# Two down-product blocks put back in two chunks, weight copies moved to ScalarE, and a new instruction order, in a four-layer attention and gated-FFN kernel

## The chip, the cores and the metric

The kernel runs on one core of a Trainium2 chip. TensorE multiplies matrices, VectorE, ScalarE and GpSimd do elementwise work, and SyncE issues the DMA transfers between HBM and the on-chip SBUF. TensorE's results go to eight PSUM banks, from which VectorE and ScalarE read them. Each engine works through its own list of instructions in order and waits at an instruction until what it needs is there. The metric is the device time of one launch in microseconds (us), lower is better; a kernel's time is the median of several runs.

## What is computed

```python
x = A_x                                              # 1 x 2048 x 576, bf16
x = x + _A_ref(_layernorm(x), A_wqkv, A_wo)
x = x + _B_ref(_layernorm(x), B_w_gate, B_w_up, B_w_down)
x = x + _A_ref(_layernorm(x), A_wqkv, A_wo)          # the same weights again
x = x + _B_ref(_layernorm(x), B_w_gate, B_w_up, B_w_down)
```

`_layernorm` is over the 576 features, without scale or shift. `_A_ref` projects to q, k and v for 32 heads of 18; token s attends to the 8 tokens s, s-2, ..., s-14, and the result goes through `wo`. `_B_ref` is `((x @ w_gate) * (x @ w_up)) @ w_down`, with an inner width F of 4608 and no nonlinearity. In tiles of 128 there are 16 token tiles and 36 f tiles; 576 features are four full tiles and a rest of 64.

## The kernel before

**Chunks.** The work goes through in chunks of tokens, called j in the code. Chunk 0 is the first token tile of the first attention layer, chunk 1 the second tile; chunks 2, 3 and 4 are pairs of tiles (256 tokens); the rest are pairs too, combined into stages of 512 tokens for the FFN. While TensorE works on the FFN of one chunk (or stage), the attention of later chunks is fitted in: `IN_GU` (L1466) says at which unit of a chunk's FFN which chunk's projection begins.

**Attention** (`attention`, L563). `head` (L441) makes the layernorm: statistics on VectorE (L455, L457) or ScalarE, `rstd` on ScalarE (L461, L462), and the apply on ScalarE (L473, L474) or on VectorE (L479). `LN1_V` and `LN2_V` say for which chunks VectorE does the apply of the first and the second layernorm. The projection is L638 for chunks 0 and 1 and L590 for the others. Scores are VectorE products of q and shifted k (L784), summed over the head by matmuls with a selection matrix `Esel` (L800) for chunks 0 and 1, or by a trip through DRAM (`s_dram`, L846, L849). The softmax is VectorE and ScalarE work (L827 to L895) and ends in the weights `a_c`. For chunks below 4 these are spread over the heads' rows by matmuls (L908) and copied to `ab`; for the later ones `a_c` goes out to `a_dram` (L921) and comes back in four pieces as `ab` (L924), on SyncE's queue. Then the a·v products: for chunk 0 pairs of offsets (L939), summed by TensorE (L979, L980) and scaled by 1/sum (L1004, L1008; the sum's matmuls stand behind product number `SPZ`); for the others one product and one sum per offset on VectorE (L954 or L957, and L963), or in pairs where the chunk is in `PAIR`. The output product with `wo` is L512 for chunks 0 and 1 and L1027 for the others, followed by the residual (L1033) and the second layernorm (`head` again; for chunks 0 and 1 `tail_fast` L500, statistics at L515).

**Weights.** In the first layer the columns of `wqkv` are put in another order on the chip (`permute`, L360). The value columns come last (`late_v`, L384): five large copies of 128 x 512 elements, one for each tile of 128 features, on the engine that `VENG` names, and five small ones on GpSimd; all are L373.

**FFN.** A unit (`g_unit`, L1136) is two to four f tiles of gate and up: full tiles at L1144, the rest of 64 features at L1154. ScalarE copies the gate result (L1085) or the up result (L1087), VectorE multiplies (L1079, L1101), and the product stays in SBUF as `hb` or in spare buffers. `Down` (L1163) multiplies with `w_down`: `block` (L1189) takes two f tiles and, for each token tile, issues a matmul of 512 columns (L1204) and one of 64 (L1205) per f tile; `fetch` (L1172) loads the weights in a ring of six buffers `wd` (L317), always a fixed number of blocks ahead; `close` (L1216) adds the sums to the residual. `first_pair` (L1309) does chunks 0 and 1 together, `small` (L1355) chunks 2, 3 and 4, `big` (L1386) the later stages. In `small`, chunks 3 and 4 (`inter`) have 18 units and 18 blocks, and the blocks run along with the units: before unit u = 4, 6, ..., 16 stand blocks u-4 and u-3, which are blocks 0 to 13. The loop after the last unit begins at nu - 2 = 16, so blocks 14 and 15 (f tiles 28 to 31 of 36) are left out of the down product of these two chunks, although their gate and up products are made and their weights loaded:

```python
        for u in range(nu):
            begin_units(in_gu.get(u, ()), push)
            if inter and u % 2 == 0 and u > 2:
                for b in (u - 4, u - 3):
                    dn.block(b)
            push(g_unit(range(u * fpu, (u + 1) * fpu), xT, xk, n, hblk[homes[u]], f"hm{homes[u]}", True))
        push()
        for b in range(nu - 2 if inter else 0, NFT // 2):
```

**The order.** Nothing of the order is written by hand. Every step is an `op` of `Plan` (L21) with an engine, an estimated cost, the tiles that it reads and writes, and a priority. `run` picks, again and again, the operation that could start earliest by these estimates (then by priority, then by age), appends it to its engine's list, and moves the estimated clock of that engine. Operations of chunk 0 are marked `first`: another operation is taken only if it would not delay one of those that are ready (`soon`), with an allowance per engine (`wait`). Gaps on TensorE before the first FFN matmul are filled with up to 44 dummy matmuls (`warm`, L1041 to L1043). So a change in costs, priorities or rules can move any instruction on any engine.

Of the kernel before, what the change touches and what calls it, by code (L numbers as in the profile page):

```python
# [20 lines left out]
class Plan:  # L21
# [52 lines left out]
    def run(self, slots):  # L74
        clock = {e: 0.0 for e in self.LAT}
        dma = 0.0
        free = {k: [(0.0, i) for i in range(v)] for k, v in slots.items()}
        cand = [o for o in self.ops if o.n == 0]
        done = 0
        while cand:  # L80
            best, found, soon = None, [], {}
            for o in cand:
                t = 0.0
                for p in o.deps:
                    e = p.ready if p.eng != o.eng or p.nbytes and p in o.data else p.end
                    if e > t:
                        t = e
                t += o.margin
                if o.hold is not None:
                    f = free[o.hold]  # L90
                    if not f:
                        continue
                    t = max(t, min(f)[0])
                if o.pair is not None:
                    if len(free["unit"]) < len(o.pair):
                        continue
                    f = sorted(free["unit"])[:len(o.pair)]
                    t = max([t, f[0][0]] + [x[0] + 150 - o.lead for x in f[1:]])
                if o.need is not None:
                    t = max(t, o.need["at"])  # L100
                t = max(t, clock[o.eng])
                found.append(((t, o.prio, o.idx), o))
                if o.first:
                    soon[o.eng] = min(t, soon.get(o.eng, t))
            for key, o in sorted(found, key=lambda x: x[0]) if self.warm is not None else ():
                if o.first or soon.get(o.eng, 1e12) >= key[0] + o.cost - self.wait.get(o.eng, 0):
                    best = (key, o)
                    break
            if best is None and found:
                best = min(found, key=lambda x: x[0])  # L110
            assert best is not None, "the plan is stuck"
            (t, _, _), o = best
            cand.remove(o)
            if o.hold is not None:
                got = min(free[o.hold])
                free[o.hold].remove(got)
                o.use["slot"] = got[1]
            if o.pair is not None:
                for u in o.pair:
                    got = min(free["unit"])  # L120
                    free["unit"].remove(got)
                    u["at"], u["slot"] = got
            if o.eng == "PE" and self.warm is not None:
                if o is self.cool:
                    self.warm = None
                else:
                    self.warm(min(44, int(max(0, t - clock["PE"] - 100) / 100)))
            o.end = t + o.cost
            clock[o.eng] = o.end
            o.ready = o.end + o.lat  # L130
            if o.nbytes:
                dma = max(dma, o.end) + o.nbytes / (330.0 if dma < 60000 else 250.0)
                o.ready = dma + o.land
# [12 lines left out]
        assert done == len(self.ops)  # L146
# [3 lines left out]
def kernel(  # L150
# [32 lines left out]

    NWD = 6
    KENG = {1: ("ACT", "ACT"), 2: ("ACT", "DVE"), 3: ("ACT", "ACT"), 4: ("ACT", "POOL")}
    VENG = ('POOL', 'POOL', 'ACT', 'ACT', 'ACT')
    LN1_PE, LN2_PE, ATT_PE, LN2_V, L1_LATE, MG, MGD = 3, 2, 4, 3, 4, 200, 2500
    LN1_V = (0, 1, 2)
    LN1_S, LN2_S = (), (2, 3, 4, 5)
    SPZ, TREE, PAIR, HPAIR = 3, (1,), (0,), 1  # L190
    RAW = 2
    WAIT = {"PE": 1e+09, "DVE": 1e+09, "ACT": 1e+09}
    PRE, SUM_PE = '', 2
# [362 lines left out]
        b, o = order_sc.index((la, t0 // NSC)) % 2, t0 % NSC  # L556
        return xnT_B[b][:, :, o * P:(o + nst) * P], [f"xB{b}_{o + i}" for i in range(nst)]

    LN1P = {1: 1.6, 2: 2, 3: 3, 4: 3, 5: 2.5, 6: 1.5, 7: 3, 8: 3}
    ATP = {1: 2.5, 2: 2.5, 3: 2.5, 4: 1.5, 5: 1.5, 6: 1.5}  # L560
    LPP = {1: 3, 2: 1.5, 3: 1.5, 4: 2, 5: 2, 6: 3}

    def attention(j, la, t0, nst, units=None, pre=""):  # L563
        fast = j == 0
# [367 lines left out]
        def pr_(i):  # L932
            return late["prod"][i][:, :, :, 0:n]
# [22 lines left out]
            abw = late["ab"][:, :, 0:W * sq].rearrange("p j (w s) -> p j w s", w=W)[:, :, i_].unsqueeze(1).to_broadcast([P, KT, 4, sq])  # L956
            nc.vector.tensor_tensor(js(dst), js(vs), abw, op=ALU.mult)  # L957
        for i_ in range(0 if j in PAIR else W):
            o = op("DVE", 60 + 3 * n, lambda i_=i_: one_v(i_), r=vk + abk, w=[f"pq{i_ % 2}"] if i_ else ok, prio=prio,
                   margin=0 if on_pe or i_ else 800 if j < 5 else 3500)  # L960
            pl.also(o, ["prod1"])
            if i_:
                op("DVE", 60 + 3 * n, lambda i_=i_: nc.vector.tensor_tensor(oT[:, :, 0:n], oT[:, :, 0:n], pr_(1)[:, i_ % 2], op=ALU.add),  # L963
                   r=[f"pq{i_ % 2}"], w=ok, prio=prio)
        for g in range(W // 2 if j in PAIR and not fast else 0):
            to = 1 if g or not tree else 0
# [388 lines left out]
    def small(j, inter, in_gu, in_d):  # L1355
        self_pair["on"] = HPAIR and not inter
        la, t0, nst = seq[j]
        n, fpu = nst * P, 4 // nst
        nu = NFT // fpu
        homes = [14 + u % 4 for u in range(nu)] if inter else [*range(9, 14), *range(9), *range(14, 18)]  # L1360

        def lhs(ft, i):
            o = (ft % fpu) * n + i * P
            return hblk[homes[ft // fpu]][:, o:o + P]
        dn = Down(t0, nst, list(range(NFT)), lhs, lambda ft, i: f"hm{homes[ft // fpu]}", la == n_al - 1, False, 2)
        dn.fetch(len(wd_ring))
        push = pusher(2, 1) if inter else pusher(3)
        marks["ld"], marks["ld1"] = marks.get("ld1"), chain["pe"]
        xT, xk = place(la, t0, nst)
        if j > 2:  # L1370
            next(gens[j], None)
        if j == 3:
            hand_over("pa", (1,))
# [4 lines that stand above are left out]
                    dn.block(b)  # L1378
            push(g_unit(range(u * fpu, (u + 1) * fpu), xT, xk, n, hblk[homes[u]], f"hm{homes[u]}", True))
        push()  # L1380
        for b in range(nu - 2 if inter else 0, NFT // 2):
            insert_d(in_d.get(b, ()))
            dn.block(b)
        dn.close()
# [78 lines left out]
        else:  # L1463
            next(gens[2], None)
    pl.first = False
    IN_GU, IN_D = {0: {3: [2]}, 2: {0: [3], 8: [4]}, 3: {0: [5], 9: [6]}}, {}  # L1466
    first_pair(IN_GU[0], IN_D.get(0, {}))
    for j in (2, 3, 4):
        small(j, j > 2, IN_GU.get(j, {}), IN_D.get(j, {}))
# [38 lines left out]
```

## Time and profile before

| what | us |
|---|---|
| median of 3 runs | 1047.61 |
| all runs | 1047.61, 1046.82, 1049.3 |
| the profiled execution | 1049.22 |
| its span in the profile | 1047.4 |

The busy times on the profile's page are 1027.5 us for TensorE, 716.7 us for VectorE, 459.3 us for ScalarE and 13.5 us for GpSimd; the time between the span and the execution's own time, 1.8 us, is outside the profile.

How rows are read. In a timeline a row has the start and the duration in us, engine, line, operation, what is written and read, the shapes and the number of instructions merged into it; in brackets at the end stands how long the engine was idle before it and what ended that. Matmuls overlap, so their pitch is read from start to start and not from the duration. A waits row has total, number and longest. A row of a stretch has its ends and length, the busy time and count of TensorE, its weight loads, VectorE, ScalarE and GpSimd, the granted TensorE clock, the DMA share and GB/s. SPq is SyncE's DMA issue.

### The profile page before, as it was taken

What the parts mean: (1) busy time and instruction counts of PE and PEld (TensorE: products, weight loads), DVE (VectorE), ACT (ScalarE), POOL (GpSimd) and SP (SyncE); (2) the same over time, 40 slices, a digit from 0 to 9 for tenths busy, and PEclk for the clock granted to TensorE, in tenths of its full rate; (3) what the DMA queues carried; (4) which work ended last, traced back from release to release, by engine and by line L of the source; (5) the groups of instructions that cost most, each with busy time, mean ns of one, the idle gap of its engine ahead of it and who ended that gap; (6) DMA issues with size and microseconds to landing.
All of it is one profiled execution on the core that took longest, in us unless ns stands there. A gap on an engine that the chain in (4) does not pass through costs nothing.

```text
span 1047.4 us, 19571 instructions
## 1 busy us (share of the span) xinstructions
PE 1027.5 (98%) x7890; PEld 597.6 (57%) x8008; DVE 716.7 (68%) x1327; ACT 459.3 (44%) x935; POOL 13.5 (1%) x51
## 2 busy tenths in 40 slices
PE   7999999999999999999999999999999999999998
PEld 6886876776765445554455544564455644554444
DVE  8886787877849886497776968579684696832211
ACT  5564764644745651354424543154531444214420
POOL 4000000000000000000000000000000000000000
PEclk9999999999999999999999999999999999999999
DMA  8918218355653715355143641525436342454212
GB/s 264 333 40 195 61 42 241 78 138 171 153 146 101 209 30 158 115 153 183 38 137 93 188 134 49 158 69 181 133 85 156 100 164 88 118 155 136 69 49 88
DMA packets 142539, 136.16 MB, mean 130 GB/s; under 512 B 46064, under 2 KB 140144, under 8 KB 142448
## 3 DMA queue, kind: packets, MB, share of 16 engines
q1 hardware_dynamic: 142448, 134.91, 44.7%
q8 instruction: 62, 1.02, 0.4%
q14 instruction: 29, 0.24, 0.1%
HBM read 114.49 MB, written 10.88 MB: 120 GB/s over the span
## 4 chain that ended last, share of the span: by engine, by line
PE 95%; DMA 2%; issue 1%; DVE 1%; SPq 1%; POOL 0%; ACT 0%; DVEq 0%
PE pu L1144 19%; PE pg L1144 18%; PE pu L1204 9%; PE pg L1204 7%; PE pa L1144 6%; PE pg L590 5%; PE pu L590 5%; PE acct L1144 5%; PE pa L1204 4%; PE pu L1154 3%; PE pg L1154 2%; PE pg L1205 2%; PE acct L1204 1%; PE acct L1027 1%; PE pu L1205 1%; PE pu L1027 1%
## 5 line engine op out<-in xcount | busy, mean ns | idle before, releaser
L1144 PEld LDWEIGHTS <-reg 128*128 128x128 bf16 x3072 | 277.9, 98 | 222.1 <-issue 24.2
L1144 PE MATMUL pu<-xnT_B,reg 128*128 128x512 bf16 (+2 forms) x1282 | 226.1, 315 | 1.5 <-issue 0.5
L1144 PE MATMUL pg<-xnT_B,reg 128*128 128x512 bf16 (+2 forms) x1192 | 213.7, 318 | 1.1 <-issue 0.3
L1204 PEld LDWEIGHTS <-reg 128*128 128x128 bf16 x864 | 84.5, 98 | 98.2
L1101 DVE TENSOR_TENSOR reg<-reg,g_sb 128x512 bf16<-128x512 bf16 x144 | 60.0, 419 | 90.5 <-ACT reg L1087 90.0
L1085 ACT CAST g_sb<-pu 128x512 bf16<-128x512 f32 x119 | 70.0, 589 | 87.8 <-PE pg L1154 41.0
L590 PEld LDWEIGHTS <-wqkv 128*128 128x128 bf16 (+1 forms) x1050 | 88.0, 97 | 34.3 <-issue 18.4
L784 DVE TENSOR_TENSOR prod<-qT,kT 128x2560 bf16<-128x2560 bf16 (+1 forms) x68 | 97.1, 1431 | 10.0 <-ACT kT L711 8.9
L1085 ACT CAST g_sb<-pg 128x512 bf16<-128x512 f32 x100 | 58.9, 590 | 96.4 <-PE pu L1154 37.7
L963 DVE TENSOR_TENSOR qT<-qT,prod 128x1280 bf16<-128x1280 bf16 (+1 forms) x112 | 89.8, 801 | 2.7
L1205 PEld LDWEIGHTS <-reg 128*128 128x128 bf16 x864 | 84.7, 98 | 1.9
L957 DVE TENSOR_TENSOR prod<-vT,ab 128x1280 bf16<-128x1280 bf16 x91 | 73.9, 818 | 4.8 <-DMA ab<-a_dram 4.8
L1144 PE MATMUL pa<-xnT_B,reg 128*128 128x512 bf16 (+1 forms) x325 | 75.0, 356 | 0.2
L461 ACT ACTIVATE rstd<-mv,eps_t 128x2 f32<-128x2 f32 (+1 forms) x32 | 9.5, 296 | 148.4 <-DVE mv L457 148.0
L590 PE MATMUL pg<-xnT_A,wqkv 128*128 128x256 bf16 (+1 forms) x495 | 71.7, 273 | 0.1
L590 PE MATMUL pu<-xnT_A,wqkv 128*128 128x256 bf16 (+1 forms) x465 | 70.5, 273 | 0.0
L1204 PE MATMUL pu<-wd,reg 128*128 128x512 bf16 x259 | 70.5, 380 | 0.0
L1154 PE MATMUL pg<-xnT_B,reg 64*128 64x512 bf16 (+2 forms) x302 | 62.7, 317 | 0.4
L1154 PE MATMUL pu<-xnT_B,reg 64*128 64x512 bf16 (+2 forms) x327 | 61.5, 315 | 0.3
L1144 PE MATMUL acct<-xnT_B,reg 128*128 128x512 bf16 (+1 forms) x217 | 56.6, 375 | 0.6 <-issue 0.2
L1205 PE MATMUL pg<-wd,reg 128*128 128x64 bf16 x264 | 50.9, 193 | 0.8
L1154 PEld LDWEIGHTS <-reg 64*128 64x128 bf16 x768 | 29.9, 94 | 36.0 <-issue 24.0
(256 smaller groups left out, 1489.8 us busy)
## 6 DMA issues: line engine op xcount, KB each, us to landing
wd<-in_B_w_down_dram SPq DMA_DIRECT2D x152, 288.0 KB, 3.2
reg<-in_B_w_gate_dram SPq DMA_DIRECT2D x24, 768.0 KB, 4.6
reg<-in_B_w_up_dram SPq DMA_DIRECT2D x24, 768.0 KB, 6.2
reg<-in_B_w_down_dram SPq DMA_DIRECT2D x28, 288.0 KB, 3.2
s_dram<-s SPq DMA_DIRECT2D x13, 512.0 KB, 3.2
rg<-s_dram SPq DMA_DIRECT2D x52, 128.0 KB, 3.0
ab<-a_dram SPq DMA_DIRECT2D x52, 128.0 KB, 2.8
reg<-in_B_w_gate_dram SPq DMA_DIRECT2D x24, 96.0 KB, 5.5
```

The costliest lines, as they stand in the source:

```text
L461: nc.scalar.activation(rstd[:, 0:nst], mv[:, 0:nst, 1], ACT.Ln, bias=eps_t[:], scale=1.0 / D if act else 1.0)
L590: nc.tensor.matmul(ring[use[p_]["slot"]][0:m, e * n:(e + 1) * n], lhsT=wqkv[r_, k, c0:c0 + m], rhs=xnT_A[r_, k, 0:n], start=start, stop=st ...
L784: nc.vector.tensor_tensor(late["prod"][lp(p_)][:, :, :, 0:n], q2, k2, op=ALU.mult)
L957: nc.vector.tensor_tensor(js(dst), js(vs), abw, op=ALU.mult)
L963: op("DVE", 60 + 3 * n, lambda i_=i_: nc.vector.tensor_tensor(oT[:, :, 0:n], oT[:, :, 0:n], pr_(1)[:, i_ % 2], op=ALU.add), r=[f"pq{i_ % 2 ...
L1027: nc.tensor.matmul(b()[:, 0:HD], lhsT=oT[:, t, i * P:(i + 1) * P], rhs=wo_p[:, t, hh * HD:(hh + 1) * HD], start=(t == 0), stop=(t == KT - 1))
L1085: op("ACT", 590, lambda: nc.scalar.copy(g_sb[gs][:, 0:ul], bk(0)[:, 0:ul]), r=[keys[0]], w=[f"g{gs}"], prio=0, **fg)
L1101: op("DVE", 410, lambda: nc.vector.tensor_tensor(dst, dst, g_sb[gs][:, 0:ul], op=ALU.mult), r=[f"g{gs}"], w=[dk], prio=0)
L1144: nc.tensor.matmul(ring[use[q]["slot"]][:, e * n:(e + 1) * n], lhsT=w_[:, k], rhs=xT[:, k], start=(first and k == 0 and e == 0), stop=(las ...
L1154: nc.tensor.matmul(ring[use[q]["slot"]][:, e * n:(e + 1) * n], lhsT=w_[r_], rhs=xT[r_, KF], start=(fresh and e == 0), stop=not fresh, skip ...
L1204: nc.tensor.matmul(bank_of(i)[:, 0:cut], lhsT=lhs, rhs=wt[:, ft % 2, 0:cut], start=first and not plus, stop=last_)
L1205: nc.tensor.matmul(tail_of(i), lhsT=lhs, rhs=wt[:, ft % 2, cut:D], start=(first and not plus and (self.fin or i == 0)), stop=last_, skip_g ...
```

## The change

1. **Blocks put back**: the loop after the units begins at nu - 4 = 14 for chunks 3 and 4, so that blocks 14 and 15 are multiplied: 8 more matmuls of 512 columns and 8 of 64 for each of the two chunks. Loads stay as many.
2. **Copies**: all five large copies of the value weights are ScalarE's; before, the first two were GpSimd's.
3. **Layernorm**: the second apply of chunk 2 goes from VectorE to ScalarE (`LN2_V` 3 to 2).
4. **Chunk 0 and 1**: the matmuls of chunk 0's softmax sum stand behind its second product instead of its fourth (`SPZ`); chunk 1's a·v is done in pairs of offsets (`PAIR`): 4 products, 3 sums of 1280 elements and a last one of 640 in place of 8 products and 7 sums of 640. `L1_LATE` 4 to 2 names which of chunk 1's score products (L784, by its pair of feature tiles) is held until chunk 0's FFN input is on its way (L806).
5. **Order**: new estimated costs for the a·v steps, new priorities (`LN1P`, `ATP`, `LPP`), chunk 4's projection begun one unit earlier (unit 7), and a new rule in `run`: for chunk 0's operations that are not yet issued, ready or not, it estimates the earliest start along their chain, so that other work is kept from delaying those too.

In the new lists TensorE has 5 fewer dummy matmuls and 32 more of the down product; the three groups of score sums of chunk 1 that stood ahead of the first FFN matmul stand behind it; chunk 2's `wo` product stands behind 54 pairs of the running down product instead of 34; and the store of `a_c` to `a_dram` in chunk 3's FFN stands behind four loads of `wd` instead of six.

```diff
@@ Plan.run
         cand = [o for o in self.ops if o.n == 0]
+        lead, gone = [o for o in self.ops if o.first], set()
...
                 if o.first:
                     soon[o.eng] = min(t, soon.get(o.eng, t))
+            if self.warm is not None:
+                est = {}
+                for o in lead:
+                    t = 0.0
+                    for p in o.deps | o.order:
+                        e = p.end + p.lat if p in gone else est.get(p, 0.0)
+                        t = e if e > t else t
+                    soon[o.eng] = min(max(t, clock[o.eng]), soon.get(o.eng, 1e12))
+                    est[o] = t + o.cost + o.lat
...
             cand.remove(o)
+            gone.add(o)
+            if o.first:
+                lead.remove(o)
@@ settings
-    VENG = ('POOL', 'POOL', 'ACT', 'ACT', 'ACT')
-    LN1_PE, LN2_PE, ATT_PE, LN2_V, L1_LATE, MG, MGD = 3, 2, 4, 3, 4, 200, 2500
+    VENG = ('ACT', 'ACT', 'ACT', 'ACT', 'ACT')
+    LN1_PE, LN2_PE, ATT_PE, LN2_V, L1_LATE, MG, MGD = 3, 2, 4, 2, 2, 200, 2500
...
-    SPZ, TREE, PAIR, HPAIR = 3, (1,), (0,), 1
+    SPZ, TREE, PAIR, HPAIR = 1, (1,), (0, 1), 1
...
-    LN1P = {1: 1.6, 2: 2, 3: 3, 4: 3, 5: 2.5, 6: 1.5, 7: 3, 8: 3}
-    ATP = {1: 2.5, 2: 2.5, 3: 2.5, 4: 1.5, 5: 1.5, 6: 1.5}
-    LPP = {1: 3, 2: 1.5, 3: 1.5, 4: 2, 5: 2, 6: 3}
+    LN1P = {1: 2.5, 2: 1.5, 3: 1.5, 4: 2, 5: 3, 6: 1, 7: 1.5, 8: 3}
+    ATP = {1: 3, 2: 3, 3: 2.5, 4: 3, 5: 2.5, 6: 2}
+    LPP = {1: 2, 2: 3, 3: 3, 4: 1.5, 5: 3, 6: 2.5}
@@ attention, a·v one offset at a time (product, and sum)
-            o = op("DVE", 60 + 3 * n, lambda i_=i_: one_v(i_), ...
+            o = op("DVE", 80 + 2.7 * n, lambda i_=i_: one_v(i_), ...
-                op("DVE", 60 + 3 * n, lambda i_=i_: nc.vector.tensor_tensor(oT[:, :, 0:n], ...
+                op("DVE", 80 + 2.7 * n, lambda i_=i_: nc.vector.tensor_tensor(oT[:, :, 0:n], ...
@@ small
-        for b in range(nu - 2 if inter else 0, NFT // 2):
+        for b in range(nu - 4 if inter else 0, NFT // 2):
@@ projections inside the FFN
-    IN_GU, IN_D = {0: {3: [2]}, 2: {0: [3], 8: [4]}, 3: {0: [5], 9: [6]}}, {}
+    IN_GU, IN_D = {0: {3: [2]}, 2: {0: [3], 7: [4]}, 3: {0: [5], 9: [6]}}, {}
```

More of the change, by code (lines that the diff above doesn't have):

```diff
@@ L958, in attention @@
         for i_ in range(0 if j in PAIR else W):
-            o = op("DVE", 60 + 3 * n, lambda i_=i_: one_v(i_), r=vk + abk, w=[f"pq{i_ % 2}"] if i_ else ok, prio=prio,
+            o = op("DVE", 80 + 2.7 * n, lambda i_=i_: one_v(i_), r=vk + abk, w=[f"pq{i_ % 2}"] if i_ else ok, prio=prio,
                    margin=0 if on_pe or i_ else 800 if j < 5 else 3500)
@@ L962, in attention @@
             if i_:
-                op("DVE", 60 + 3 * n, lambda i_=i_: nc.vector.tensor_tensor(oT[:, :, 0:n], oT[:, :, 0:n], pr_(1)[:, i_ % 2], op=ALU.add),
+                op("DVE", 80 + 2.7 * n, lambda i_=i_: nc.vector.tensor_tensor(oT[:, :, 0:n], oT[:, :, 0:n], pr_(1)[:, i_ % 2], op=ALU.add),
                    r=[f"pq{i_ % 2}"], w=ok, prio=prio)
```

## The prediction

> **What bounds the kernel now.** I read the shares of the chain that ended last, then the list of what TensorE waited for, then the busy time by stretch.
>
> ```profile
> PE 95%; DMA 2%; issue 1%; DVE 1%; SPq 1%; POOL 0%; ACT 0%; DVEq 0%
> ```
> ```profile
> PE pg L638 <- POOL wqkv L373: 2.7, 2, 2.2
> PE pa L1204 <- DVE hb L1079: 2.0, 1, 2.0
> ...
> PE pg L638 <- ACT xnT_A L495: 1.0, 1, 1.0
> ...
> PE pg L1204 <- DVE hb L1079: 0.2, 1, 0.2
> ```
> ```profile
> 0.00:34.00 34.00, 27.24 (x468) 23.15 (x469) 28.51 (x64) 18.69 (x42) 12.94 (x43) 0.95 0.94 280
> ...
> 175.00:250.00 75.00, 72.61 (x670) 53.93 (x676) 58.78 (x104) 39.58 (x84) 0.00 (x0) 1.00 0.54 142
> 250.00:330.00 80.00, 79.27 (x672) 55.52 (x681) 59.28 (x124) 46.72 (x98) 0.00 (x0) 1.00 0.49 121
> 330.00:1020.00 690.00, 684.42 (x4332) 343.19 (x4416) 459.97 (x845) 271.46 (x537) 0.00 (x0) 1.00 0.41 122
> ```
>
> 95% of the chain is TensorE. A waits line gives microseconds in total, times, and the longest. A stretch line gives its length, then busy time of TensorE, its weight loads, VectorE, ScalarE and GpSimd, the granted clock and DMA. TensorE is idle 6.8 us of the first 34 us and about 5.6 us of the 690 us after 330. So the time is TensorE's own work plus two places: the start, where one chain of small steps runs before the first gated FFN matmul, and one wait of 2.0 us at L1204. An added matmul costs its full pitch unless it falls into one of these holes; a gain on VectorE or ScalarE counts only in them.
>
> **The blocks put back (L1381).** The loop after the units begins at block 14 instead of 16, for chunks 3 and 4. A block is 2 f tiles by 2 token tiles, each one matmul of 512 and one of 64 columns: 8 pairs for two blocks, 16 in all. The price is read from another two-block step of chunk 3, on TensorE's own timeline:
>
> ```profile
> 218.29 0.38 PE L1204 MATMUL pa<-wd,hb 128*128 128x512 bf16 x1
> ...
> 220.25 1.04 PE L1144 MATMUL pu<-xnT_B,reg 128*128 128x256 bf16 x8
> ```
>
> From 218.29 to 220.25 is 1.96 us for 8 pairs, 0.245 us a pair. Sixteen pairs: **+3.92 us** if nothing covers them. The weights of these blocks are loaded already, so no transfer is added.
>
> At the end of chunk 3 the new pairs come right after the last unit's matmuls, ahead of blocks 16 and 17, and there is the hole (TensorE, then VectorE):
>
> ```profile
> 241.83 1.04 PE L1144 MATMUL pu<-xnT_B,reg 128*128 128x256 bf16 x8
> 244.84 0.39 PE L1204 MATMUL pa<-wd,hb 128*128 128x512 bf16 x1 [1.97 <-DVE hb L1079]
> ```
> ```profile
> 237.42 0.43 DVE L1079 TENSOR_TENSOR hb<-hb,g_sb 128x512 bf16<-128x512 bf16 x1 [1.16 <-ACT hb L1087]
> 242.16 1.56 DVE L957 TENSOR_TENSOR prod<-vT,ab 128x1280 bf16<-128x1280 bf16 x2 [4.31 <-DMA ab<-a_dram]
> 243.63 0.82 DVE L957 TENSOR_TENSOR qT<-vT,ab 128x1280 bf16<-128x1280 bf16 x1
> 244.37 0.42 DVE L1079 TENSOR_TENSOR hb<-hb,g_sb 128x512 bf16<-128x512 bf16 x1
> ```
>
> The 237.42 product is unit 15's, so blocks 14 and 15 have their operands 5 us before TensorE is free at 242.87. Unit 16's product, at 244.37, stands on VectorE behind three multiplications that waited 4.31 us for the attention weights. So the two blocks fill 1.96 of 1.97 us: **−1.97 us**, even if the wait's end stays where it is. At the end of chunk 4 the same happens to the smaller wait:
>
> ```profile
> 304.11 0.39 PE L1204 MATMUL pg<-wd,hb 128*128 128x512 bf16 x1 [0.16 <-DVE hb L1079]
> ```
>
> **−0.16 us.** Is 244.8 itself moved? The weights came late through SyncE's queue (VectorE, then the queue, then the chain):
>
> ```profile
> 229.34 0.69 DVE L895 TENSOR_TENSOR a_c<-Lt,zs 128x512 bf16<-128x512 f32 x1
> ```
> ```profile
> 219.47 13.08 SPq L317 DMA_DIRECT2D wd<-in_B_w_down_dram  x6
> 232.64 0.42 SPq L921 DMA_DIRECT2D a_dram<-a_c  x1
> ```
> ```profile
> 236.91 5.22 DMA ab<-a_dram
> ```
>
> `a_c` was ready at 230.03, its store issued at 232.64: six loads of down weights stood ahead for 13.08 us. Since nothing read the weights of the missing blocks, their buffers were loaded again at once; in the changed order only four such loads stand ahead of the store. So I expect the store some 2.5 us earlier and the wait gone with room. If the queue stays as it is, the blocks still just cover it; if the store came later, each us would cost one. Range of both blocks together: +1.8 (covered, my value) to +3.92.
>
> **The start.** The large value-weight copies go from GpSimd to ScalarE (L373). GpSimd's, ScalarE's, TensorE's and VectorE's rows:
>
> ```profile
> 11.46 4.51 POOL L373 COPY wqkv<-xl 128x64 bf16<-128x64 bf16 x7 [1.49 <-DMA xl<-in_A_wqkv_dram]
> ```
> ```profile
> 11.65 3.13 ACT L373 COPY wqkv<-xl 128x512 bf16<-128x512 bf16 x3
> ```
> ```profile
> 14.39 0.40 PE L638 MATMUL pg<-xnT_A,wqkv 128*128 128x128 bf16 x4 [2.21 <-POOL wqkv L373]
> ...
> 17.50 0.31 PE L638 MATMUL pu<-xnT_A,wqkv 128*128 128x128 bf16 x1
> ...
> 33.48 1.07 PE L1144 MATMUL pg<-xnT_B,reg 128*128 128x128 bf16 x16
> ```
> ```profile
> 19.18 0.42 DVE L840 TENSOR_REDUCE mx<-acct 128x32 f32<-128x256 f32 x1 [0.63 <-PE acct L800]
> ...
> 24.49 0.63 DVE L479 TENSOR_SCALAR xn<-xf,mv,rstd 128x576 bf16<-128x576 bf16 x2
> ...
> 27.94 0.29 DVE L1004 TENSOR_TENSOR oT<-pg,Lt 128x128 bf16<-128x128 f32 x1 [0.70 <-PE pg L980]
> 28.39 0.76 DVE L1008 TENSOR_TENSOR oT<-acct,Lt 128x256 bf16<-128x256 f32 x2 [0.16 <-issue]
> 29.07 0.82 DVE L784 TENSOR_TENSOR prod<-qT,kT 128x1280 bf16<-128x1280 bf16 x1
> ```
>
> Three copies on ScalarE took 3.13 us, 1.04 each; five end at 11.65 + 5.2 = 16.9. The first is there at 12.7 instead of after 14, so the 2.21 us wait goes, but the last one now sets the end: the value product's last piece starts at about 16.9 instead of 17.5, and the softmax's first reduction at 18.6 instead of 19.18: 0.6 us. On VectorE, the layernorm apply at 24.49 (0.63 us, L479) stands between chunk 0's a·v products; in the changed order it comes behind the last of them, where VectorE had a pause of 0.70 us anyway: 0.65 us. And L784 for chunk 1 leaves its place behind L1008, 0.82 us, of which I count 0.35, since the wo product of TensorE lies beside it. Sum: **−1.6 us** to the first FFN matmul at L1144. Three groups of 20 score-sum matmuls (L800), 0.26 us each, that stand ahead of 33.48 move behind it too, so the first L1144 itself should come 2.4 us earlier, and 0.8 of that is paid later. Bounds: 0 (the last copy, at 16.9, could hold everything) to −3.5 (2.7 of waits and 0.82).
>
> A clock effect lies in this stretch:
>
> ```profile
> 16.54 0.63 PE L638 MATMUL pg<-xnT_A,wqkv 128*128 128x128 bf16 x4
> ...
> 21.30 0.39 PE L638 MATMUL pg<-xnT_A,wqkv 128*128 128x128 bf16 x4
> ```
> ```profile
> 16.00:16.50 0.50, 0.47 (x5) 0.47 (x6) 0.50 (x1) 0.00 (x0) 0.00 (x0) 0.50 0.32 55
> ...
> 20.00:20.50 0.50, 0.00 (x0) 0.00 (x0) 0.50 (x3) 0.50 (x2) 0.00 (x0) 1.00 1.07 390
> ```
>
> The granted clock is 0.50 at 16.0 and 1.00 at 20.0; four matmuls take 0.63 us in the one and 0.39 in the other. The Trainium skill, "TensorE: Matmul & The Clock Gate", Part 1, says that the gate looks at free-running windows of about 3.4 us and gives half rate after an idle one. That agrees with these rows, and it speaks against the change: a new order moves the idle pieces against the windows. I keep it as a rival.
>
> **The middle: chunk 2, and the rest of the new order.** Chunk 1's eight products and seven sums (640 columns) become four, three and one of double width, as many elements; its a·v ends within 1 us of before, 0.6 us ahead of need: 0 ± 0.6. Chunk 4's projection is begun a unit earlier: 0, TensorE is full there and does the same work. One second layernorm apply of chunk 2 goes from VectorE to ScalarE, about 1.4 us ahead of its reader: 0. What I can't cost at nothing is the wo product of chunk 2 (VectorE, then TensorE):
>
> ```profile
> 75.02 0.82 DVE L954 TENSOR_TENSOR qT<-vT,ab 128x1280 bf16<-128x1280 bf16 x1 [0.28 <-ACT ab L711]
> ...
> 82.94 0.69 DVE L1079 TENSOR_TENSOR xnT_B<-xnT_B,g_sb 128x1024 bf16<-128x1024 bf16 x1 [0.52 <-ACT xnT_B L1087]
> ...
> 88.32 0.82 DVE L963 TENSOR_TENSOR qT<-qT,prod 128x1280 bf16<-128x1280 bf16 x1
> ```
> ```profile
> 90.45 0.78 PE L1027 MATMUL acct<-wo_p,qT 128*128 128x288 bf16 x5
> ```
>
> Before, the 15 products and sums began at 75.02 among the FFN products and ended at 89.1, 1.3 us ahead of L1027. In the changed order they stand behind the last FFN product (about 82, 1.6 us earlier than 83.6): 15 × 0.79 = 11.9 gives 93.9. L1027 is moved behind 20 more pairs of the down product, 4.9 us: 90.45 − 1.6 + 4.9 = 93.75. Slack is −0.1: I take +0.3 us, with 0 to +3 (four of the 0.79 us steps later) as its range.
>
> **Sum**: 3.92 − 1.97 − 0.16 − 1.6 + 0.3 = +0.5 us. On the profiled execution, 1049.22 us with a span of 1047.4, that gives 1049.7; the three runs have their median at 1047.61 (1046.82 to 1049.3), 1.6 below it, so the forecast is **1048.1 us**.
>
> **The rivals.** *Chunk 2's wo product becomes the wait* (slower). For it: VectorE is the fuller engine there, and 11.9 us now follow each other with no slack at L1027. Against: 20 more pairs stand ahead of L1027, which cover the later start but for 0.1 us. It decides once `qT` is done later than 93.75; each VectorE step pushed ahead costs 0.79, and layernorm, on ScalarE now, hands it on. Three or four steps, 2.4 to 3.2: about 1050.8. *The half clock comes again* within chunk 0's a·v stretch, since TensorE's new order has a half-idle piece at 19 to 22 us. The 0.63 against 0.39 above, over 3.4 us, is some 1.3 to 1.7 us: 1049.6. The Trainium skill ("TensorE: Matmul & The Clock Gate", Part 1) has this by its rule. *The start gives all* (faster): both waits for GpSimd, 2.7 us, and the 0.82 come through, −3.5 instead of −1.6, and chunk 2's wo product waits for nothing, 0 instead of +0.3: 1048.1 − 1.9 − 0.3 = 1045.9; with one or two of the pauses left behind the softmax (0.70 at 27.94) filled too, 1045.2. For it: the chain is serial; against: the last copy at 16.9. *The blocks don't fit the hole*, because the changed queue holds unit 15's or the weights' arrival: 3.92 in full and a wait behind, about 1050.2.
>
> **How the numbers follow.** Forecast 1048.1, own range 1046.7 to 1049.5: 0.48. Wo product of chunk 2: 0.20. Start gives all: 0.20. Half clock: 0.06. Blocks not covered: 0.06. A measurement can tell about 0.2%, 2.1 us, from no change: 1045.5 to 1049.7. Faster: two thirds of the start's case and a small tail of the forecast, 0.16. Slower: nine tenths of the wo product's case, most of the uncovered blocks, half of the clock's case and a tail of the forecast, 0.30. The rest, 0.54, is within. The range is 1044.8 to 1051.2: 1 in 10 is left out on each side.
>
> **What would show it.** Right: L1204 and L1205 with 16 more pairs; no wait of TensorE for L1079 near 243 us; the store of `a_c` near 230 and no row of six down-weight loads before it; first FFN matmul (L1144's line) near 31.1 us; the wait for GpSimd's copies gone, and none above 0.5 us for chunk 2's `qT`. Wrong: a wait at the wo product near 93 us; a granted clock of 0.50 after 22 us; a first FFN matmul later than 33; a wait of over 1 us at the end of chunk 3; or a changed pitch after 330 us, which no term here allows.

## The result, and the profile after

Against before on the same chip the change makes the kernel slower: 1051.35 us against 1048.05 us (medians of 8 runs each), a ratio of 1.0026 with a 95% interval of 1.0015 to 1.0037. The unchanged pair was measured once more (e11): 1050.17 against 1047.55, ratio 1.0021 (1.0012 to 1.0030). So it costs 2.2 to 2.7 us, where the forecast was +0.5. Among the runs of e11 and of before beside it whose mean granted clock was 1.000 the difference is larger, 3.6 us, since 15 of the 21 runs of before had a lower clock and only 4 of the 11 of the changed kernel (0.999). The two profiled executions show little of it: 1049.77 us with a span of 1048.0, against 1049.22 and 1047.4.

First, what TensorE waited for after (total, times, longest; the line numbers are 13 higher, so L1217 is the old L1204, L1040 the old L1027, L386 the old L373).

```profile
...
PE acct L813 <- DVE prod L797: 1.2, 2, 1.0
PE pa L1056 <- ACT xnT_A L508: 1.1, 1, 1.1
PE pu L603 <- issue: 1.0, 1, 1.0
...
PE pu L921 <- ACT a_c L884: 0.6, 1, 0.6
PE pg L1157 <- DMA reg<-in_B_w_gate_dram: 0.5, 1, 0.5
PE pu L651 <- POOL wqkv L386: 0.4, 1, 0.4
...
```

The wait for GpSimd's copies (2.7 us) is down to 0.4, both waits for L1079 are gone, and no wait for chunk 2's `wo` product has come. New is 1.0 us of "issue" at a projection matmul, time in which TensorE waited for nothing that the profile names. The same stretches as before:

```profile
0.00:34.00 34.00, 28.45 (x514) 24.78 (x514) 26.16 (x64) 21.72 (x46) 11.16 (x41) 1.00 0.98 288
...
175.00:250.00 75.00, 74.58 (x688) 55.30 (x695) 60.62 (x106) 40.20 (x86) 0.00 (x0) 1.00 0.51 145
250.00:330.00 80.00, 79.37 (x673) 55.09 (x683) 55.66 (x119) 45.71 (x96) 0.00 (x0) 1.00 0.51 117
330.00:1020.00 690.00, 684.32 (x4330) 343.17 (x4415) 458.88 (x845) 271.44 (x537) 0.00 (x0) 1.00 0.42 122
```

From 330 us on TensorE's busy time is the same to 0.1 us. At the end of chunk 3's FFN, SyncE's queue, VectorE and TensorE show the mechanism that was forecast: `a_c` is ready at 228.88 (the end of the L908 row), its store goes out at once with no loads ahead of it, the products follow 4 us earlier than in the profile before, and blocks 14 to 17 run through without a pause (these are the first and the last rows of their 512-column matmuls in TensorE's timeline).

```profile
228.92 0.34 SPq L934 DMA_DIRECT2D a_dram<-a_c  x1
```
```profile
228.19 0.69 DVE L908 TENSOR_TENSOR a_c<-Lt,zs 128x512 bf16<-128x512 f32 x1
...
238.00 1.56 DVE L970 TENSOR_TENSOR prod<-vT,ab 128x1280 bf16<-128x1280 bf16 x2 [1.18 <-DMA ab<-a_dram]
```
```profile
241.68 0.38 PE L1217 MATMUL pa<-wd,hb 128*128 128x512 bf16 x1
...
245.11 0.38 PE L1217 MATMUL pg<-wd,hb 128*128 128x512 bf16 x1
```

Of chunk 2's a·v, the first and the last VectorE row, and TensorE's `wo` product behind it:

```profile
82.13 0.82 DVE L967 TENSOR_TENSOR qT<-vT,ab 128x1280 bf16<-128x1280 bf16 x1
...
93.28 0.82 DVE L976 TENSOR_TENSOR qT<-qT,prod 128x1280 bf16<-128x1280 bf16 x1
```
```profile
94.33 0.78 PE L1040 MATMUL acct<-wo_p,qT 128*128 128x288 bf16 x5
```

The start of the changed kernel, ScalarE's copies, VectorE's softmax and the first FFN matmul:

```profile
11.88 5.22 ACT L386 COPY wqkv<-xl 128x512 bf16<-128x512 bf16 x5
```
```profile
17.07 0.40 DVE L853 TENSOR_REDUCE mx<-acct 128x32 f32<-128x256 f32 x1
...
25.33 0.74 DVE L1021 TENSOR_TENSOR oT<-pu,Lt 128x256 bf16<-128x256 f32 x2
27.38 0.47 DVE L528 BATCH_NORM_STATS2 st<-acct 128x6 f32<-128x288 f32 x1 [1.30 <-PE acct L525]
```
```profile
30.17 1.05 PE L1157 MATMUL pg<-xnT_B,reg 128*128 128x128 bf16 x16 [0.46 <-DMA reg<-in_B_w_gate_dram]
```

Five copies in 5.22 us, as worked out; the softmax comes 2.1 us earlier than before, the first FFN matmul 3.3 us earlier. Then where did the gain go? To compare kernels below, I use one ruler: the start of the n-th full FFN matmul (L1144's line) in each trace. Matmul 513 comes after the start and the FFN of chunks 0 and 1, 1025 near the end of chunk 3's units, 1401 in the stage behind chunk 4; the two places of the change lie between the last two.

| profile | 1st | 513th | 1025th | 1401st | 1025 to 1401 |
|---|---|---|---|---|---|
| before | 33.48 | 113.44 | 238.56 | 334.39 | 95.83 |
| before again, e9 | 33.47 | 113.43 | 238.55 | 332.47 | 93.92 |
| before again, e10 | 33.68 | 113.65 | 238.77 | 333.03 | 94.26 |
| after | 30.17 | 112.42 | 237.54 | 334.87 | 97.33 |
| after again, e11 | 30.89 | 112.57 | 238.02 | 335.56 | 97.54 |

From matmul 1401 to the last one every kernel takes 673.40 us, to 0.01. (Some matmul records are missing from the traces; counted by weight loads, of which none is missing, the differences between the kernels in the last column are the same to 0.01.)

### The profile page after: what moved, and what is told of

Read it like the earlier page. It is cut to its first block, busy times and chain, and to the rows that moved or that the text cites. A ratio compares the mean times of both kernels' runs of the same rounds, so it can differ in the third digit from the quotient of the medians.

```text
span 1048.0 us, 19612 instructions
## 1 busy us (share of the span) xinstructions
PE 1030.1 (98%) x7917; PEld 599.3 (57%) x8035; DVE 710.7 (68%) x1317; ACT 463.6 (44%) x941; POOL 11.7 (1%) x49
## 4 chain that ended last, share of the span: by engine, by line
PE 96%; DMA 2%; issue 1%; POOL 1%; SPq 0%; DVE 0%; ACT 0%; POOLq 0%
PE pu L1157 19%; PE pg L1157 18%; PE pg L1217 9%; PE pu L1217 6%; PE pa L1157 6%; PE pg L603 5%; PE pu L603 5%; PE acct L1157 4%; PE pa L1217 4%; PE acct L1217 3%; PE pu L1167 3%; PE pg L1167 3%; PE pg L1218 2%; PE pu L1040 1%; PE pu L1218 1%; DMA reg<-in_B_w_gate_dram 1%
## 5 line engine op out<-in xcount | busy, mean ns | idle before, releaser
L1157 PE MATMUL pg<-xnT_B,reg 128*128 128x512 bf16 (+2 forms) x1200 | 220.6, 319 | 1.9 <-issue 0.6
L1217 PEld LDWEIGHTS <-reg 128*128 128x128 bf16 x864 | 84.5, 98 | 98.2
L1098 ACT CAST g_sb<-pu 128x512 bf16<-128x512 f32 x113 | 66.5, 590 | 104.2 <-PE pg L1167 59.1
L1098 ACT CAST g_sb<-pg 128x512 bf16<-128x512 f32 x111 | 65.5, 590 | 76.5 <-PE pu L1167 44.1
L976 DVE TENSOR_TENSOR qT<-qT,prod 128x1280 bf16<-128x1280 bf16 x105 | 86.3, 822 | 2.3
L1167 PE MATMUL pg<-xnT_B,reg 64*128 64x512 bf16 (+2 forms) x305 | 68.2, 319 | 0.6
L1217 PE MATMUL pg<-wd,reg 128*128 128x512 bf16 (+1 forms) x233 | 62.7, 369 | 0.0
L1218 PE MATMUL pg<-wd,reg 128*128 128x64 bf16 x320 | 61.7, 193 | 0.7
L1157 PE MATMUL acct<-xnT_B,reg 128*128 128x512 bf16 (+1 forms) x213 | 54.1, 375 | 0.1
L1167 PEld LDWEIGHTS <-reg 64*128 64x128 bf16 x768 | 29.9, 94 | 36.4 <-issue 24.6
```

What stands on the lines that cost most here:

```text
L976: op("DVE", 80 + 2.7 * n, lambda i_=i_: nc.vector.tensor_tensor(oT[:, :, 0:n], oT[:, :, 0:n], pr_(1)[:, i_ % 2], op=ALU.add), r=[f"pq{i_ % ...
L1098: op("ACT", 590, lambda: nc.scalar.copy(g_sb[gs][:, 0:ul], bk(0)[:, 0:ul]), r=[keys[0]], w=[f"g{gs}"], prio=0, **fg)
L1157: nc.tensor.matmul(ring[use[q]["slot"]][:, e * n:(e + 1) * n], lhsT=w_[:, k], rhs=xT[:, k], start=(first and k == 0 and e == 0), stop=(las ...
L1167: nc.tensor.matmul(ring[use[q]["slot"]][:, e * n:(e + 1) * n], lhsT=w_[r_], rhs=xT[r_, KF], start=(fresh and e == 0), stop=not fresh, skip ...
L1217: nc.tensor.matmul(bank_of(i)[:, 0:cut], lhsT=lhs, rhs=wt[:, ft % 2, 0:cut], start=first and not plus, stop=last_)
L1218: nc.tensor.matmul(tail_of(i), lhsT=lhs, rhs=wt[:, ft % 2, cut:D], start=(first and not plus and (self.fin or i == 0)), stop=last_, skip_g ...
```

## The experiments

The theory at the outset: the start's gain is real only against executions whose clock was halved there, and one of the two pairs of blocks is covered. The rival: the start gains what was forecast, and the blocks cost more.

**e1: the blocks alone.** The kernel before with

```diff
-        for b in range(nu - 2 if inter else 0, NFT // 2):
+        for b in range(nu - 4 if inter else 0, NFT // 2):
```

> The kernel before with only the loop start changed, so that blocks 14 and 15 are multiplied in chunks 3 and 4. Theory (one of the two places is covered): at the end of chunk 3 the 1.96 us fill the wait of 1.97 us, at the end of chunk 4 there is only 0.16 us to fill, so +1.8 us on before, ratio 1.0017. Rival (the blocks are not covered): +3.9 us, ratio 1.0037, with a wait at L1204 still there near 244 us.

Measured: 1050.34 us against 1048.32, ratio 1.0020 (1.0007 to 1.0033), +2.1 us. In the profile the wait near 244 us is gone, and the store of `a_c` goes out at 229.43, right behind `a_c` (228.72 + 0.69). So the queue's order follows from the blocks alone, as forecast. The interval holds +1.8 and leaves the rival's +3.9 out. This speaks for the theory only for now: e8 to e10 and e12 below show what the blocks cost and how much was covered. (In e1, and in e8 and e12 below, the planner also moves other work behind the added blocks.)

**e2: all but the blocks.** The changed kernel with

```diff
-        for b in range(nu - 4 if inter else 0, NFT // 2):
+        for b in range(nu - 2 if inter else 0, NFT // 2):
```

> The changed kernel with the loop start of before: blocks 14 and 15 of the down product of chunks 3 and 4 are left out again, all else as changed. Theory (the new start gains only against executions in which the clock was halved at the start, as in the profiled one of before): full-clock runs 0.5 to 1.0 us slower than full-clock runs of before, so ratio 1.000 to 1.001. Rival (the start gains 1.6 us as forecast, and the blocks cost more): 1.2 us or more faster than before, ratio 0.9988.

This leaves blocks 14 and 15 out of chunks 3 and 4, as before does. Measured: 1047.98 against 1048.32, ratio 0.9995 (0.9983 to 1.0007): neither a clear gain nor a loss; the interval holds both theories' values. Its profile has the wait of 1.0 us at the same projection matmul, and at the end of chunk 3 a wait of 0.76 us, for down weights, where before's profile had 1.97. The runs at a mean clock of 1.000 do tell the two apart: the six of e2 have a median of 1048.07 and begin at 1047.65, the ten of before have 1046.76 and end at 1047.18. So at equal clock the new order without the blocks is 1.3 us slower. The theory has the direction right there, with 0.5 to 1.0, and the rival, 1.2 us faster, fails; over all runs the two are level because before lost clock in 25 of its 35 runs.

**e3 and e4: more dummy matmuls**, in before and in after:

```diff
-                    self.warm(min(44, int(max(0, t - clock["PE"] - 100) / 100)))
+                    self.warm(min(80, int(max(0, t - clock["PE"] - 100) / 65)))
```

> The kernel before with more dummy matmuls in the same gaps of TensorE (one for each 65 ns of an estimated gap instead of one for each 100, at most 80). Theory (the runs of before near 1049.3 us are those whose clock was halved for one window of 3.4 us at the start): fewer or no runs with a mean clock of 0.998, and those with a full clock near 1047.4; median 0.3 to 0.8 us lower. Rival (the two groups of runs come from something else, or the dummies stand in the way): the same spread of 1046.8 to 1049.8, or all runs later by the dummies.

> The changed kernel with the same denser dummy matmuls. Theory (clock): no run with a mean clock of 0.998, and the median falls from 1051.35 to near 1050.0, where the full-clock runs of the changed kernel are. Rival (the runs near 1051.5 come from the late instruction fetch that the profile shows as a wait of 1.0 us near 39.8 us, which two runs at full clock speak for): the runs near 1051.4 stay, at a clock of 1.0.

Measured: 1050.99 (ratio 1.0025, 1.0013 to 1.0037) and 1051.22 (1.0022, 1.0011 to 1.0033). The mean clock was 1.000 in 8 of e3's 12 runs and in all 12 of e4's, so the runs agree with dummies holding it up, but the kernels are no faster for it: e3's 513th matmul stands at 114.47 us at full clock, before's at 113.44 with a halved one, and e4's at 114.11, after's at 112.42. The rival's second half holds, the dummies stand in the way. What the clock costs can be read from the 35 runs of before beside these: median 1046.76 for the 10 at a mean clock of 1.000, 1048.47 for the 12 at 0.998, and 1050.45 for the 6 at 0.995. A step down goes with 1.7 to 2.0 us here, and with 0.8 to 2.5 in the two later sets of before. It doesn't hold run by run: in e5 below the five runs at 0.998 are no slower than the five at 1.000 (1049.43 and 1049.85), and e10, at 1.000, took longer than e9 at 0.998. And both profiles have the wait for "issue", of 0.91 us, e3's in before's order.

**e5: fewer dummies.** The wait for "issue" stands at one and the same place in the profiles of four kernels (after, e2, e3, e4), the 1217th row of TensorE's list (weight loads counted), in whatever line that is. The changed kernel with

```diff
-                    self.warm(min(44, int(max(0, t - clock["PE"] - 100) / 100)))
+                    m = min(44, int(max(0, t - clock["PE"] - 100) / 100), 96 - self.warmed)
+                    self.warmed += m
+                    self.warm(m)
```

> The changed kernel without the last 16 of its 112 dummy matmuls (those after 20.47 us), all other work in the same order. Theory (TensorE's instructions from its 1217th row on arrive at a set time, about 39.8 us, since in the four profiles with a wait of 0.9 to 1.0 us near 38 to 40 us it stands at just that row; 32 rows less ahead of it bring TensorE there about 1.8 us of matmuls later): no such wait, full-clock runs 1.0 us faster than those of the changed kernel (1050.31), near 1049.4. Rival (the wait belongs to a time or to the weights that are loaded then): it stays, and the time is within 0.4 us of the changed kernel's; the clock may be halved more often.

Measured: 1049.85 against 1048.41, ratio 1.0012 (1.0002 to 1.0021); the changed kernel's ratios are 1.0026 and 1.0021, so by the medians e5 is about 1 us ahead of it, but the intervals overlap. The wait is gone (TensorE's timelines of after, then of e5, around that row; e5's line numbers are 3 higher):

```profile
38.45 0.38 PE L603 MATMUL pu<-xnT_A,wqkv 128*128 128x256 bf16 x2
39.84 0.38 PE L603 MATMUL pu<-xnT_A,wqkv 128*128 128x256 bf16 x2 [1.00 <-issue]
```
```profile
39.85 0.60 PE L606 MATMUL pg<-xnT_A,wqkv 128*128 128x256 bf16 x4
40.29 0.60 PE L606 MATMUL pu<-xnT_A,wqkv 128*128 128x256 bf16 x4
40.73 0.38 PE L924 MATMUL pa<-a_c,Bsel 128*128 128x256 bf16 x2
```

The theory is right about the wait. The gain of 1.0 us is not shown: at a mean clock of 1.000 e5 has 1049.85 (5 runs) against the changed kernel's 1050.31 (5 runs), half of it, and in e5's profile, whose clock was halved for one window, the 513th matmul stands at 112.65, no earlier than after's 112.42. Of the kernels that compute all blocks e5 has the lowest ratio, but its interval overlaps e1's too; it is still behind before, which leaves two blocks of two chunks out.

**e6 and e7: the copies.** e6 is the changed kernel with the first two copies on GpSimd, e7 the kernel before with all five on ScalarE:

```diff
-    VENG = ('ACT', 'ACT', 'ACT', 'ACT', 'ACT')
+    VENG = ('POOL', 'POOL', 'ACT', 'ACT', 'ACT')
```

```diff
-    VENG = ('POOL', 'POOL', 'ACT', 'ACT', 'ACT')
+    VENG = ('ACT', 'ACT', 'ACT', 'ACT', 'ACT')
```

> The changed kernel with the first two large value-weight copies on GpSimd again. Theory (the copies on ScalarE shorten the waits at the start by 1 to 2 us, but most of what the profiled kernel before lost there was its halved clock): full-clock runs 0 to 0.6 us slower than the changed kernel's 1050.3, and more runs with a mean clock of 0.998 or less, as TensorE waits longer in one piece. Rival (forecast: the copies give at least the 0.6 us of the softmax and the whole waits of 2.7 us count): 1.5 us or more slower at full clock.

> The kernel before with all five large value-weight copies on ScalarE, nothing else. Theory: full-clock runs within 0.6 us of before's 1046.8, fewer runs at 0.998 or less, so that the median falls by some 0.5 to 1 us. Rival: 1.6 us faster at full clock too.

Measured: e6 1053.82 (1.0053, 1.0041 to 1.0065), by the ratios 2.8 to 3.4 us behind the changed kernel; its 513th matmul stands at 115.17, 2.75 later than after's. A part of that is the clock, which was below 1.000 in four of its five runs, the profiled one among them, as the theory said it would be; the one run at 1.000 took 1052.56, 2.25 more than the changed kernel's median there. So the theory's 0 to 0.6 us fell, and the forecast's reading is borne out, by one run at full clock: in the new order the copies on ScalarE are worth some 2 to 3 us, near the 2.7 that the waits said. (The planner also gave the other steps of the start another order.) e7, though, took 1066.69 (1.0173, 1.0160 to 1.0186). Neither theory had that; its 513th matmul stands at 132.44, 19.0 later than in the profile of before. The copies change the estimated clocks, and the planner put the scores of chunk 2 (45.9 to 59.0 us) in the middle of chunk 1's a·v on VectorE, while TensorE's list has chunk 2's score sums and spreads ahead of the rest (TensorE's timeline, then stretches of e7):

```profile
55.91 0.30 PE L800 MATMUL pa<-s,Esel 128*32 128x128 bf16 x4 [2.93 <-DVE s L794]
59.08 0.30 PE L800 MATMUL pa<-s,Esel 128*32 128x128 bf16 x4 [2.87 <-DVE s L794]
64.90 0.59 PE L908 MATMUL acct<-a_c,Bsel 128*128 128x512 bf16 x1 [5.51 <-DVE a_c L895]
```
```profile
50.00:56.00 6.00, 3.07 (x62) 2.83 (x60) 5.76 (x10) 1.18 (x3) 0.00 (x0) 0.97 0.85 292
56.00:70.00 14.00, 4.28 (x21) 2.06 (x21) 13.09 (x29) 3.88 (x9) 0.00 (x0) 0.53 0.00 1
```

TensorE did 4.28 us of work in 14, and the granted clock fell to 0.53. So part 2 of the change and its new rule, priorities and costs are not separate gains: the copies alone, under the old planner's settings, lose 18 us. Which of the planner's settings prevents that was not tried.

**e8: the blocks of chunk 3 alone**, in before:

```diff
-        for b in range(nu - 2 if inter else 0, NFT // 2):
+        for b in range((nu - 4 if j == 3 else nu - 2) if inter else 0, NFT // 2):
```

> The kernel before with blocks 14 and 15 put back in chunk 3 alone; chunk 4 still leaves them out. Theory (the wait of 1.97 us at the end of chunk 3 takes them): within 0.3 us of before, and no wait at L1204 near 243 us; all of what e1 lost is then chunk 4's. Rival (both chunks cost alike): about half of what both blocks cost together in e1, 1.0 us or more.

This kernel leaves blocks 14 and 15 of chunk 4 out. Measured: 1049.84 against 1048.41, ratio 1.0016 (1.0005 to 1.0027), by the ratio +1.7 us; the rival's value. Yet by the ruler 1025 to 1401 takes 95.54 us, 0.29 less than the profile of before, and the wait near 243 us is gone. The profile agreed with the theory and the times did not. That left one suspect: the wait of 1.97 us in the profile of before.

**e9 and e10: the kernel before, profiled twice more**, with no edit.

> The kernel before, unchanged, for another profile. Theory (the wait at the end of chunk 3 is as long as the store and reload of the weights happen to take, so one profile of 1.97 us overstates the hole; two other kernels without blocks 14 and 15 showed 1.62 and 0.76 us): the wait at L1204 near 243 us is under 1.5 us. Rival (the hole is always there in full, and the 1.5 us that blocks in chunk 3 cost come from elsewhere): 1.9 to 2.0 us again.

> The kernel before, unchanged, a third profile, as e9: theory, the wait at L1204 near 243 us differs from e9's and from 1.97 us by some tenths of a us or more, with the landing of the reload; rival, 1.9 to 2.0 us again.

Measured: 1047.27 and 1047.83 us in the profiled executions (one each). Ahead of block 16, where the first profile had 1.97 us, TensorE waited 0.41 in e10 and not at all in e9; e9 has 0.15 us ahead of the next block, 17. This is e9's TensorE, from the first matmul of block 16 to the first of block 17 (the row before that one ends at 243.85):

```profile
242.69 0.39 PE L1204 MATMUL pa<-wd,hb 128*128 128x512 bf16 x1
...
243.66 0.19 PE L1205 MATMUL pu<-wd,hb 128*128 128x64 bf16 x1
244.00 0.39 PE L1204 MATMUL pa<-wd,hb 128*128 128x512 bf16 x1
```

From start to start these four pairs take 1.31 us, where four at 0.245 would take 0.98: the idle time of 0.15 us costs 0.33 in pitch. At the end of chunk 4 the wait of 0.16 costs the same (four pairs from 302.81 to 304.11 in the profile of before, 1.30 us).

The chain of waits of e10 shows why the hole is smaller:

```profile
232.43 2.85 DMA a_dram<-a_c
...
236.61 4.17 DMA ab<-a_dram
```

The store went out 0.2 us earlier than in the first profile (232.64), behind the same loads; but the reload landed at 240.78 instead of 242.13. In e9 VectorE's products began at 240.01:

```profile
240.01 1.56 DVE L957 TENSOR_TENSOR prod<-vT,ab 128x1280 bf16<-128x1280 bf16 x2 [2.18 <-DMA ab<-a_dram]
```

So 2 us in the landing of one reload decide between a hole of 1.97 and one of 0.15. The five profiles in before's order without chunk 3's blocks have, as the longest wait at these two blocks, 1.97 (before), 0.15 (e9), 0.41 (e10), 1.62 (e3) and 0.16 (e12). By the ruler (1025 to 1401) before takes 93.92 and 94.26, and the blocks of chunk 3 cost 95.54 − 93.92 = 1.62 us. The theory holds: the hole is as long as the store and reload happen to take. From the store's issue to VectorE's first product it is 9.5 us in the profile of before and 7.6 to 8.4 in the other four; in e3 the store itself went out late, at 234.72. A long hole is not an accident of a single profile, since two of the five have 1.6 us or more and three 0.4 or less; why the reload takes longer in some executions was not tried.

**e11: the changed kernel again**, with no edit.

> The changed kernel, unchanged, beside fresh runs of before on this chip. Theory: full-clock runs 3 to 4 us behind full-clock runs of before (1.0 us is the wait before row 1217, which is in this profile too at 0.9 to 1.1 us; the rest the blocks), the medians of all runs 2.3 to 3 us apart since the halved clock is rarer than before. Rival (the 1.0 us wait was a chance of one profile): no wait over 0.4 us near 40 us.

Measured, as above: 1050.17 against 1047.55, ratio 1.0021. At a mean clock of 1.000 it is 1050.37 (7 runs) against 1046.74 (6 runs), +3.6 us; over all runs only +2.2 to 2.6, since 15 of the 21 runs of before lost clock and none of its 11 fell below 0.999. The wait at row 1217 is there again, 0.58 us. The theory holds; its lower bound of 0.9 for that wait does not.

**e12: the blocks of chunk 4 alone**, in before:

```diff
-        for b in range(nu - 2 if inter else 0, NFT // 2):
+        for b in range((nu - 4 if j == 4 else nu - 2) if inter else 0, NFT // 2):
```

> The kernel before with blocks 14 and 15 put back in chunk 4 alone. Theory (only a wait of 0.16 us is there to fill): 1.96 less 0.16 is +1.8 us, with a range of 1.0 to 1.9, at equal clock, and the wait at L1204 near 243 us is as before. Rival (chunk 4's end has other slack, as e1 less e8 is only 1.1 us): +0.5 us or less.

This kernel leaves blocks 14 and 15 of chunk 3 out. Measured: 1051.00 against 1047.55, ratio 1.0024 (1.0011 to 1.0037). By the ruler 95.55 us against e9's 93.92: +1.63, within what was expected; e1 with both pairs takes 97.18, +3.26. The rival is out. By the ratio its times are 2.5 us up, which holds more than the blocks: in its profile the first FFN matmul came at 34.64, 1.2 later than e9's, with a wait of 3.0 us for GpSimd's copy, and only 2 of its 10 runs had a mean clock of 1.000.

## Why the prediction was right or wrong

The sign of the sum was right and its size too small: 2.2 to 2.7 us were lost where 0.5 was forecast, just past what was called within 0.2%. The first comparison's median, 1051.35, lies 0.15 above the range's end, the second's, 1050.17, within it; added to the 1047.61 on which the forecast stood, 2.2 to 2.7 gives 1049.8 to 1050.3, inside the range. That it lies there is in part luck: before loses clock in more of its runs, and at a mean clock of 1.000 the loss is 3.6 us. Step by step:

- **The price of the blocks** (3.92 us, 0.245 a pair): right. The 16 pairs of blocks 14 to 17 run from 241.68 to 245.60 in the profile after, 3.92 us, 0.245 each. Against e9 the blocks of both chunks cost 3.26 us by the ruler (1.62 and 1.63 in e8 and e12), which is 3.92 less twice the 0.33 us of pitch that the small waits cost. The forecast's −0.16 for chunk 4 took the idle time for the cost; it should have been −0.33.
- **The step that failed** is "so the two blocks fill 1.96 of 1.97 us: −1.97". Mechanism and queue were right: the store of `a_c` moved from 232.64 to 228.92, the wait vanished, blocks 14 to 17 run through. The size of the hole was not: 0.15 and 0.41 us in two other profiles of the same kernel. Against the profile of before the stretch cost 97.33 − 95.83 = 1.50 us, near the forecast's 1.8; against e9 and e10 it cost 3.1 to 3.4. In the sum the term of −1.97 is the one that was mis-sized: without it +0.5 becomes +2.5. The forecast's upper end for the blocks, 3.92, took in that they might not be covered, but with the wrong reason, "if the store came later". The rival that the blocks don't fit the hole, about 1050.2, came nearest in time and had a chance of only 0.06; its reason, that the changed queue holds something back, was not what happened either.
- **The start** (−1.6): right against the profiled executions, not at equal clock. Against the three profiles of before the 513th matmul comes 0.9 to 1.2 us earlier, and it would be more without the new wait of 0.6 to 1.0 us at row 1217, which no step of the forecast had. The first FFN matmul came 2.6 to 3.5 us earlier (forecast 2.4). But the times of e2 at a mean clock of 1.000 leave no gain of the new order, they are 1.3 us behind before; its profile holds the wait of 1.0 at row 1217, and by the ruler 0.7 us at the end of chunk 3 (94.61 against e9's 93.92). Two of the three profiles of before had the clock halved, and the third, e10, is slower (1047.83) than every full-clock run of before on that chip (at most 1047.18), so no profile shows how before's start runs in its faster executions. Whether the start gains anything at equal clock stays open. In the profile after one part of the way differs: the softmax came at 17.07, not 18.6, and VectorE then waited 1.30 us for TensorE's `wo` product ahead of L528, so the a·v stretch gained more and the end of it less.
- **Chunk 2's wo product** (+0.3, and the slower rival): no wait. The 15 products and sums run from 82.13 to 94.10 in the profile after, forecast 82 to 93.9, and L1040 stands at 94.33: the slack is 0.2 us where −0.1 was forecast.
- **The clock**: the second rival was on the right track, with the sign turned around. The halved clock strikes before more than after. In the profile of before it was halved from 15.8 to 19.2 us, 3.41 us long, in e5's from 21.1 to 24.6, and with each step of the mean clock the 35 runs of before were 1.7 to 2.0 us longer. That the new order's idle pieces fall better against the windows is argued, not tried by itself. The Trainium skill's "TensorE: Matmul & The Clock Gate", Part 1, has this window at 3413 ns and free-running, and these runs agree, in the length and in that the same program meets it in some executions and not in others.

Put together, for profiled executions: against e9, whose clock was halved once, the profile after has +3.4 us between matmuls 1025 and 1401, of which 3.26 are the blocks, and −1.0 up to the 513th, +2.4 in sum. That is within the 2.2 to 2.7 of the comparisons over all runs. At a mean clock of 1.000 the times are 3.6 us apart, more than the blocks' 3.26 alone, so no gain of the start is left in them.

## What to carry to other kernels

A wait that a single profile shows is the wait of that execution. Where it ends with a DMA's landing, take a second profile of the same kernel before counting on it as cover, or keep its whole length as an uncertainty: here it was 1.97, 0.41 and 0.15 us. And where a planner sets the order, one setting is not one change: the copies on ScalarE were worth some 2 to 3 us in the new order and lost 18 us in the old one. And where the clock differs from run to run, compare runs at the same clock beside all runs: e2 is level with before over all runs and 1.3 us behind it at full clock.

## What the runs showed of the hardware

TensorE's instructions arrive in blocks of 16 KB on a DMA queue of their own (the profile's "q8 instruction": 62 packets, 1.02 MB, in the profile of before, one for every 256 of TensorE's 15,898 matmuls and weight loads). The times of the fetches below are from the trace's packets of that queue. The 1217th row goes with the fourth fetch: where TensorE arrives early, it waits until 2.4 to 2.8 us after that fetch began, in whatever line it then is:

| profile | fetch begins | TensorE is at row 1217 | row 1217 starts | wait |
|---|---|---|---|---|
| after | 37.31 | 38.84 | 39.84 | 1.00 |
| e11 | 37.70 | 39.56 | 40.15 | 0.58 |
| e2 | 37.12 | 38.93 | 39.92 | 0.99 |
| e4 | 35.22 | 36.90 | 37.81 | 0.91 |
| e6 | 39.07 | 40.32 | 41.63 | 1.31 |
| e1 | 36.95 | no wait | 39.72 | 0 |
| e5 | 38.46 | no wait | 41.27 | 0 |
| before | 37.67 | no wait | 40.65 | 0 |

Of the other six profiles e3 and e7 wait too (0.91 and 0.96 us, until 2.5 us after the fetch), and e8, e9, e10 and e12 come 2.7 to 3.0 us after it and don't wait.

So at the start, where many narrow matmuls follow each other and the weights fill the DMA queues (a DMA share of 1.08 in the rows of 20 to 50 us), a faster order can outrun its own instructions, and a dummy matmul takes two rows of them, its own and its weight load's. The Trainium skill ("Runtime: NRT & Kernel Launch", Instruction fetch mechanics) has the block of 16 KiB and 256 instructions and calls the crossing mostly hidden; here it was not, by 0.6 to 1.3 us. The fetch follows TensorE's own progress: in all 14 profiles it begins 2.8 to 4.2 us after TensorE passed row 961, which is 256 rows ahead of 1217 (33.16 and 37.31 in the profile after). Further on, at row 1985, the fetch begins within 1.0 us of TensorE's passing (69.97 and 70.14 there). Why it comes 3 to 4 us late at the start, where the DMA share is highest, was not settled.
